# Performer attention and an MLP mixer on one Trainium2 core: q and k of the first two batches loaded in rows of 18 tokens

## The chip, the core and the metric

The kernel runs on one core of a Trainium2 chip. The core has a matrix engine (TensorE, called PE in the profile; its weight loads are listed apart as PEld), a vector engine (VectorE, DVE), a scalar engine (ScalarE, ACT), a general engine (GpSimd, POOL) and SyncE (SP), which here only issues DMAs. Each engine takes its instructions strictly in the order of its program. Matmul results go to eight PSUM banks, and from there ACT or DVE must copy them to SBUF. The metric is the device time of one execution in microseconds, as the median of several runs.

## The reference, cut to what matters

Eight batches of 8 heads, 576 tokens and head size 64 pass through Performer attention (128 random features) and then an MLP mixer.

```python
def phi(x):                                  # x: q or k, scaled by 64 ** -0.25
    proj = np.einsum('bhsd,md->bhsm', x, omega)
    h = proj - np.sum(x * x, -1, keepdims=True) / 2
    return np.exp(h - np.max(h, -1, keepdims=True)) / np.sqrt(m)
kv  = einsum('bhsm,bhsd->bhmd', phi(k), v);  z = phi(k).sum(axis=2)
x   = einsum('bhsm,bhmd->bhsd', phi(q), kv) / (phi(q) . z + 1e-6)     # then (B, 576, 512)
h   = relu(x.T @ w_tok1) @ w_tok2;  u = x + h.T                       # over tokens
out = u + relu(u @ w_ch1) @ w_ch2                                     # over channels, 512 -> 1536 -> 512
```

## The kernel before

Every batch goes through the same stages: transposed q and k (head dimension on the partitions), features (a matmul with omega, then an exponential on ACT, lines 628 and 640 with 499), the maxima of k's features (DVE, 652) and v scaled by them (POOL, 293), kv (PE, 673 and 682), the numerators (PE, 706 and 708), their division (DVE, 715 and 716, for some heads DVE 725 and ACT 728), token mix and channel mix. The 576 tokens are handled as 512 and a tail of 64: a transposed tile keeps 256 columns of main part and 32 columns of tail for each head, two tokens to a column.

Batches 2 to 7 get q and k transposed by DMA through a copy in DRAM. The first two batches (`NPE = 2`) are transposed on PE. For k of batch 0 the main part arrives in fp32 by four DMAs that SP and ACT issue (`load_first`, line 383). All else of these two batches comes by DMAs that POOL issues, and that turn fp32 to fp16 on the way: `load_nat` (317) takes 512 tokens of a head, four to a partition, so that one run in DRAM is 1 KB, and `load_nat_tail` (328) takes the 64 tail tokens of all eight heads. `transposes` (472) turns four heads with eight instructions of 128x128 into one bank, and one copy of 128x1024 (helper line 284) takes it out in the same order; `tail_transposes` (489) needs four instructions and one copy of 128x256 for a whole tail, which puts the columns in order as it copies.

The first batch is the head of the kernel. Its token mix is special (`token_mix_first`): per block of 128 channels a first matmul group (788, 789), a relu, a group that leaves the sum of x and the token mix transposed (800, 802), and a copy of it (tile uT, line 284 again). When three of the four uT copies are done, the first channel matmuls of batch 0 may start (944, three of four contraction blocks), and their fourth block (946) needs the last copy. From there on the channel matmuls of one batch (938, 972, 888) are work that PE can do while the next batch's attention waits for ACT and DVE.

What sets the order is written out by hand. `add` registers jobs, and `Planner.run` issues them as the list `ORDER` says; a negative number is a filler matmul (line 1013) whose result nobody reads. `SLOT` says which bank or buffer each job takes, and `MOVED` puts single jobs on another engine than the usual one. The costs and keys given to `add` no longer decide anything. So the order of a queue (POOL's DMA issues and its arithmetic, ACT, DVE, PE) is fixed, and an instruction that waits holds all behind it on that engine.

## Time and profile before

| what | value |
|---|---|
| median of 3 runs | 279.24 us (278.15 to 279.55) |
| profiled execution: its own time | 279.25 us |
| profiled execution: span from the first to the last instruction | 277.5 us |
| granted TensorE clock, mean | 0.997 |
| PE, DVE, ACT, POOL busy | 97%, 79%, 49%, 34% of the span |
| first channel matmul of batch 0 | 30.06 us |

Times in the profile count from the start of the span; 1.75 us of the execution's time lie outside of it. Busy time of PE counts a matmul until its modelled end, so that neighbours overlap: the step from one 512-column matmul to the next is read off the chain, where eight of line 938 take 1.73 us. In a line of instructions the columns are the start, the duration, the engine, the line, the operation, the tile written and the tile read, their shapes, the number merged into the line, and in brackets the engine's idle time before and what ended it. In a table of stretches each engine has its busy time, with the number of instructions in brackets, and at the end the granted clock, the DMA share and GB/s.

### The profile page before, as it was taken

Reading aid. Unit: us, or ns where it says so; the run is one execution under the profiler, and the core shown is the slowest. Engines: PE = TensorE matmul, PEld = TensorE weight load, DVE = VectorE, ACT = ScalarE, POOL = GpSimd, SP = SyncE. Lnnn points to the kernel's source line nnn. Section 1 sums busy time; section 2 is a strip of 40 time slices with the busy share of each in tenths; the row PEclk is TensorE's granted clock in tenths of the full one; section 3 lists DMA queues with packets and bytes.
Section 4 is the critical chain, followed back from the end, with each engine's and each line's share of the span. In section 5 each row is a group of like instructions: output and inputs, shape, how many; then the busy total and the mean of one; then the engine's idle time right before and its main releaser. Section 6 shows DMA issues by size and latency. Waiting matters only on the chain.

```text
span 277.5 us, 6130 instructions
## 1 busy us (share of the span) xinstructions
PE 269.2 (97%) x2459; PEld 168.2 (61%) x2459; DVE 220.4 (79%) x462; ACT 137.0 (49%) x284; POOL 93.5 (34%) x117
## 2 busy tenths in 40 slices
PE   8989999999999999999999999999999999999992
PEld 4558455445567655756676656655676477456782
DVE  2989678397996999987999799969995991595892
ACT  1988942396595337625756546635744500211200
POOL 8995782063812480076019500600042000000001
PEclk9999999999999999999999999999999999999998
DMA  7999999999999999979999997750342204030125
GB/s 189 174 201 197 208 207 177 197 184 180 204 196 122 218 169 172 192 136 166 180 183 201 234 113 118 171 123 0 102 73 83 90 6 90 0 154 0 76 99 132
DMA packets 84012, 39.66 MB, mean 143 GB/s; under 512 B 64208, under 2 KB 80528, under 8 KB 83792
## 3 DMA queue, kind: packets, MB, share of 16 engines
q0 software_dynamic: 34464, 17.74, 45.8%
q1 hardware_dynamic: 47360, 16.03, 29.1%
q10 hardware_dynamic: 2160, 5.51, 5.1%
q8 instruction: 19, 0.31, 0.5%
q14 instruction: 9, 0.07, 0.1%
HBM read 35.95 MB, written 16.52 MB: 189 GB/s over the span
## 4 chain that ended last, share of the span: by engine, by line
PE 83%; DVE 7%; DMA 4%; POOL 3%; issue 1%; DVEq 0%; POOLq 0%
PE bank L938 30%; PE bank L888 26%; PE bank L749 4%; PE bank L762 4%; DMA r<-in_k_dram 3%; PE bank L673 3%; PE bank L706 3%; PE bank L972 2%; PE bank L640 2%; PE bank L628 2%; DMA vt<-in_v_dram 1%; DVE T L448 1%; DVE km L652 1%; DVE S L293 1%; DVE u L765 1%
## 5 line engine op out<-in xcount | busy, mean ns | idle before, releaser
L938 PE MATMUL bank<-uT,wc 128*128 128x512 f16 x376 | 89.5, 379 | 0.0
L288 ACT ACTIVATE r<-bank 128x512 f16<-128x512 f32 (+1 forms) x86 | 48.2, 601 | 79.0 <-PE bank L938 66.3
L293 POOL TENSOR_TENSOR vs<-v,vs 128x512 f16<-128x512 f16 x32 | 33.6, 1057 | 92.9 <-DVE vs L654 62.8
L938 PEld LDWEIGHTS <-wc 128*128 128x128 f16 x424 | 38.6, 98 | 37.5 <-issue 0.3
L499 ACT ACTIVATE qp<-bank 128x512 f16<-128x512 f32 x64 | 36.8, 625 | 10.1 <-PE bank L640 7.3
L888 PEld LDWEIGHTS <-r 128*128 128x128 f16 x384 | 36.9, 98 | 8.0 <-issue 0.7
L652 DVE TENSOR_REDUCE km<-kp 128x8 f16<-128x1024 f16 x32 | 38.6, 1207 | 2.5 <-ACT kp L499 2.4
L499 ACT ACTIVATE kp<-bank 128x512 f16<-128x512 f32 x64 | 35.8, 615 | 6.3 <-PE bank L628 5.1
L290 DVE TENSOR_SCALAR r<-bank 128x512 f16<-128x512 f32 (+1 forms) x40 | 26.0, 669 | 7.8 <-PE bank L938 6.8
L716 DVE TENSOR_TENSOR x<-bank,rc 128x320 f16<-128x320 f32 x62 | 30.5, 491 | 2.1
L888 PEld LDWEIGHTS <-S 128*128 128x128 f16 x288 | 28.0, 98 | 5.6 <-issue 0.4
L877 DVE TENSOR_TENSOR o<-u,bank 128x512 f32<-128x512 f16 x28 | 19.0, 678 | 7.8 <-PE bank L888 7.7
L888 PE MATMUL bank<-T,r 128*128 128x256 f16 x192 | 23.8, 273 | 0.0
L888 PE MATMUL bank<-T,S 128*128 128x256 f16 x192 | 23.6, 273 | 0.1
L888 PE MATMUL bank<-wc,r 128*128 128x256 f16 x192 | 23.4, 273 | 0.0
L917 POOL DMA_DIRECT2D out_dram<-o x2 | 1.3, 645 | 61.1 <-issue 61.1
L765 DVE TENSOR_TENSOR u<-x,bank 128x512 f16<-128x512 f16 x28 | 17.6, 680 | 4.7 <-PE bank L762 4.7
L877 DVE TENSOR_TENSOR o<-o,bank 128x512 f32<-128x512 f32 (+1 forms) x27 | 16.5, 615 | 3.1 <-PE bank L888 2.6
L706 PEld LDWEIGHTS <-qp 128*128 128x128 f16 x256 | 13.8, 98 | 7.9 <-DVE kvsb L284 0.2
L706 PE MATMUL bank<-kvsb,qp 128*128 128x65 f16 x256 | 15.5, 193 | 0.0
L715 DVE RECIPROCAL rc<-bank 128x5 f32<-128x5 f32 x62 | 11.5, 185 | 4.8 <-PE bank L708 3.5
L673 PEld LDWEIGHTS <-kp 128*128 128x128 f16 x256 | 11.0, 98 | 5.2 <-DVE o L284 1.0
(117 smaller groups left out, 381.5 us busy)
## 6 DMA issues: line engine op xcount, KB each, us to landing
out_dram<-o ACTq DMA_DIRECT2D x9, 512.0 KB, 3.5
q<-in_q_dram POOLq DMA_DIRECT2D x6, 576.0 KB, 9.6
wc<-in_moe_w_ch_dram POOLq DMA_DIRECT2D x4, 768.0 KB, 13.4
k<-in_k_dram POOLq DMA_DIRECT2D x6, 512.0 KB, 8.1
v<-in_v_dram POOLq DMA_DIRECT2D x6, 512.0 KB, 10.1
out_dram<-o SPq DMA_DIRECT2D x5, 512.0 KB, 3.3
r<-in_q_dram POOLq DMA_DIRECT2D x4, 256.0 KB, 7.3
v<-in_v_dram POOLq DMA_DIRECT2D x4, 256.0 KB, 8.0
```

Of the source, the lines that this page charges most:

```text
L288: nc.scalar.activation(out=out, in_=in_, func=AF.Relu)
L290: nc.vector.tensor_relu(out=out, in_=in_)
L293: (nc.gpsimd if eng == "POOL" else nc.vector).tensor_tensor(**kw)
L499: nc.scalar.activation(out=out, in_=in_, func=AF.Exp, bias=0.0, scale=1.0)
L652: nc.vector.reduce_max(out=mx, in_=kpv, axis=AX.X)
L673: nc.tensor.matmul(ps[:, i, :], kpv[:, 2 * i + j // 2, j % 2, :], vs[:, i * NJ + j, 0 : D + 1], start=(i == 0 and j == 0), stop=False, ski ...
L706: nc.tensor.matmul(ps[:, k, j * 65 : (j + 1) * 65], st, s[:, i, 0 : D + 1], start=True, stop=True)
L716: nc.vector.tensor_tensor(out=t_x[place("x", b)][:, :, (2 * hp + hs[0]) * D : (2 * hp + hs[0] + n) * D].rearrange("p j (i d) -> p i j d", ...
L765: nc.vector.tensor_tensor(out=t_u[place("u", b)][:, j, :], in0=t_x[place("x", b)][:, j, :], in1=bank(n), op=ALU.add)
L877: nc.vector.tensor_tensor(out=o, in0=a, in1=ps, op=ALU.add)
L888: nc.tensor.matmul(ps[:, j * DH : (j + 1) * DH], a[:, cb, j * P : (j + 1) * P], w[:, cb, :], start=(bank_of(b, j0) not in held and j == j0 ...
L938: nc.tensor.matmul(ps, wc1[:, db, cb * P : (cb + 1) * P], moving(db), start=(db == 0), stop=(db == ND - 1))
```

## The change

q of batch 0, and q and k of batch 1, are no longer split into main part and tail when loaded. Four heads are 2304 tokens, and they are laid as 128 rows of 18 tokens (`RW = 18`), so that one run in DRAM is 4.5 KB and one head covers 32 partitions. Three tail loads of `load_nat_tail` go, and the one load of k of batch 1 becomes two of four heads. k of batch 0 stays as it was, with its tail.

The new function `row_transposes` takes the place of `transposes` and `tail_transposes` for them. It issues nine pairs of transposes per four heads, each from 64 partitions and 128 columns, the two of a pair on the two halves of the partitions and into two banks. Each bank holds two heads, and the copy out of it (128x576) puts the columns in order: neighbours in the output lie 64 columns apart in the bank. For k a second, small copy brings the tail columns (128x64) to the tile that the tail's matmul reads. The matmuls that read these tiles now pick tokens in steps of two columns, as they do in batches 2 to 7. Jobs that depended on one copy of four heads now depend on the copy of their two heads, and the tail's matmul (601, and 534 for batch 1) on all copies.

With it `ORDER`, `SLOT` and `MOVED` are new. In the list of before, ACT has ten exponentials of batch 1 (two of them of the tail) ahead of the copy of uT's last block, and does two of the four uT copies by then; in the new list it has nine of them, and does only that one. New on ACT ahead of it are two of the four row copies of q of batch 0, three of the four of k of batch 1, two of the four of q of batch 1, the copy of k's tail of batch 0 and one more relu; DVE no longer does these, but does the first and third uT copies, one vs product (formerly POOL's), and the other row copies. On DVE and ACT k of batch 0 is copied by two each, not three and one. On POOL the list of loads starts with the tail of k, q, the two loads of v's tail, q, v, the second half of k of batch 1, v, and its first half. On PE the first kv matmuls of batch 0 come before the transposes of batch 1, which came first; there are 22 fillers in place of 20; and two q feature groups of batch 1 that stood ahead of the first channel matmul stand behind it. Later batches have the same jobs with neighbours swapped here and there, and some relus and copies on the other of ACT and DVE.

```diff
 ORDER = [
-    6, 5, 0, 2, 3, 1, 4, 17, 15, 19, 7, 10, 13, -1, -2, -3, -4, -5, -6, -7, 49, 12, 40, 47, 8, 41, 43, 42, 48,
-    23, 44, 50, -8, 45, 11, 108, 9, 123, 110, 51, 52, 22, 125, 46, -1, -4, 71, 124, 79, 14, 53, 72, 109, 32, 93,
-    81, 57, 54, 95, 18, 55, 114, 58, 80, 30, 76, 67, 77, 20, 56, 74, -7, -7, -7, 96, 85, 73, 82, 75, 94, 97, -4,
-    111, 68, 83, 99, 126, 112, 98, 21, -2, -2, 199, 78, 129, 86, -3, 63, 128, 84, 100, -8, 87, 201, 64, 88, 16,
...
+    6, 5, 0, 2, 3, 1, 4, 16, 14, 18, 15, 7, 10, 9, -1, -2, -3, -4, -5, -6, -7, 47, 8, 45, 38, 48, 39, 12, 46,
+    40, 41, 11, 106, 42, 43, 107, 22, 108, 49, 44, 77, 13, 50, 121, 78, 112, 91, 21, 123, -8, 51, 79, 17, 52,
+    53, 28, 93, 83, -1, -4, -3, -1, 94, 122, 19, 80, 96, 54, 73, 92, 69, 55, 81, 70, 82, 95, 24, 56, 97, 71, 84,
+    -5, -8, -3, -5, -7, -7, -8, -1, 74, 109, 72, 127, 76, 98, -6, -2, 85, 75, 124, 63, 113, 86, 125, 128, 87,
+    89, 110, 99, 90, 30, 126, 114, 88, 100, 129, 20, 65, 57, 130, 111, 64, 25, 133, 131, 59, 135, 115, 31, 58,
+    132, 104, 60, 23, 134, 136, 101, 116, 61, 118, 137, 29, 102, 119, 103, 105, 33, 147, 117, 120, 139, 138,
...
 MOVED = {
-    52: "DVE", 70: "ACT", 88: "ACT", 142: "DVE", 144: "DVE", 146: "DVE", 148: "ACT", 152: "ACT", 155: "DVE",
-    158: "DVE", 176: "DVE", 178: "DVE", 182: "ACT", 192: "ACT", 216: "ACT", 244: "DVE", 258: "DVE", 288: "DVE",
-    326: "ACT", 380: "DVE", 401: "DVE", 428: "DVE", 430: "DVE", 434: "DVE", 436: "DVE", 486: "DVE", 500: "DVE",
...
+    42: "DVE", 46: "ACT", 48: "ACT", 52: "ACT", 56: "ACT", 58: "ACT", 59: "ACT", 61: "ACT", 62: "ACT", 65:
+    "ACT", 86: "ACT", 128: "DVE", 138: "DVE", 142: "DVE", 144: "DVE", 150: "ACT", 156: "DVE", 160: "DVE", 162:
+    "DVE", 164: "ACT", 172: "ACT", 176: "DVE", 180: "ACT", 214: "ACT", 286: "DVE", 324: "ACT", 378: "DVE", 399:
...
 }
...
     NPE = 2
+    RW = S * 4 // P
     c_scale = float(1.0 / math.sqrt(math.sqrt(D)))
...
         for i, w in enumerate("qk"):
-            nat[w, b] = flat(t)[:, i * H * 256 : (i + 1) * H * 256].rearrange("p (h e) -> p h e", h=H)
-        nat["t", b] = flat(t)[:, 2 * H * 256 : 2 * H * 256 + H * D].rearrange("p (i e) -> p i e", i=4)
+            nat[w, b] = flat(t)[:, 2 * i * RW * D : 2 * (i + 1) * RW * D].rearrange("p (g e) -> p g e", g=2)
+        nat["t", b] = flat(t)[:, 4 * RW * D : 4 * RW * D + H * D].rearrange("p (i e) -> p i e", i=4)
 
...
             nc.gpsimd.dma_start(
-                out=nat[w, b][:, h0:h1, :],
-                in_=src[w][b, h0:h1, 0:SM, :].rearrange("h (p j) d -> p h (j d)", j=NJ),
+                out=nat[w, b][:, h0 // 4, :],
+                in_=src[w][b, h0:h1].rearrange("h s d -> (h s d)").rearrange("(p f) -> p f", p=P),
             )
...
     load_nat(0, "q", 4, 8, -8.5)
-    load_nat_tail(0, "q", -8.48)
     load_v(0, -8.45, (), 4, 8)
...
     load_wc1(0)
-    load_nat(1, "k", 0, 8, -9.61)
-    load_nat_tail(1, "k", -3.48)
+    load_nat(1, "k", 0, 4, -9.61)
+    load_nat(1, "k", 4, 8, -9.61)
     load_v_tail(1, -3.46)
     load_wc1(1)
-    load_nat_tail(1, "q", -3.44)
     load_w1t(0, -3.42)
...
         t = (t_qT if w == "q" else t_kT)[place(w + "T", b)]
-        return (t[:, 0 : H * R] if w == "k" and b >= NPE else t).rearrange("p (h r) -> p h r", h=H)
+        return (t[:, 0 : H * R] if w == "k" and b != 1 else t).rearrange("p (h r) -> p h r", h=H)
 
...
 
-    def transposes(b, w, h0, h1, key, on_act=False, key_out=None):
-        name = ("t", w, b, h0)
-        first = b == 0 and w == "k"
+    def transposes(b, h0, h1, key, on_act=False, key_out=None):
+        name, w = ("t", "k", b, h0), "k"
         def go():
-            ps = bank(name) if first else bank16(name)
-            what, ident = (first_k, ident32) if first else (nat[w, b], ident16)
+            ps = bank(name)
             for i in range(2 * (h1 - h0)):
                 h, pr = h0 + i // 2, i % 2
-                nc.tensor.transpose(ps[:, i * P : (i + 1) * P], what[:, h, pr * P : (pr + 1) * P], ident)
+                nc.tensor.transpose(ps[:, i * P : (i + 1) * P], first_k[:, h, pr * P : (pr + 1) * P], ident32)
         def out_():
             n = h1 - h0
-            ps = (bank(name) if first else bank16(name))[:, 0 : n * R].rearrange("p (h r) -> p h r", h=n)
-            copy(eng, rows_of(b, w)[:, h0:h1, 0:R], ps)
+            copy(eng, rows_of(b, w)[:, h0:h1, 0:R], bank(name)[:, 0 : n * R].rearrange("p (h r) -> p h r", h=n))
         take = [("bank", name), (w + "T", b)]
-        t = add("PE", mm(2 * (h1 - h0), P) * (2 if first else 1), key, go, deps=[ld[w, b, h0], j_ident32 if first else j_ident], take=take)
+        t = add("PE", mm(2 * (h1 - h0), P) * 2, key, go, deps=[ld[w, b, h0], j_ident32], take=take)
         eng = engine("ACT" if on_act else "DVE")
...
             tr[w, b, h] = e
+
+    def row_transposes(b, w, g, key, on_act=False, key_out=None):
+        names = [("t", w, b, g, o) for o in range(2)]
+        def rows():
+            for i in range(RW // 2):
+                for o in range(2):
+                    p = slice(o * ST, (o + 1) * ST)
+                    nc.tensor.transpose(bank16(names[o])[:, i * ST : (i + 1) * ST], nat[w, b][p, g, i * P : (i + 1) * P], ident16[p, p])
+        t = add("PE", mm(9, 64), key, rows, deps=[ld[w, b, 4 * g], j_ident], take=[*[("bank", n) for n in names], (w + "T", b)], rows=True)
+        for o in range(2):
+            eng = engine("ACT" if on_act else "DVE")
+            def rows_out(o=o, eng=eng):
+                h = 4 * g + 2 * o
+                to = rows_of(b, w)[:, h : h + 2, :]
+                copy(eng, to.rearrange("p h (c i) -> p h c i", i=RW // 2), bank16(names[o])[:, 0 : 2 * RA].rearrange("p (i h c) -> p h c i", i=RW // 2, h=2))
+                if w == "k":
+                    copy(eng, t_ktt[place("ktt", b)][:, h * RT : (h + 2) * RT].rearrange("p (h r) -> p h r", h=2), to[:, :, R:RA])
+            e = add(eng, 0.38 if w == "q" else 0.48, key if key_out is None else key_out, rows_out, deps=[t], take=[("ktt", b)] if w == "k" else [], give=[("bank", names[o])])
+            for h in range(2):
+                tr[w, b, 4 * g + 2 * o + h] = e
 
...
             ps = bank16(name)[:, 0 : H * RT].rearrange("p (i h g) -> p h g i", i=4, h=H)
-            to = t_ktt[place("ktt", b)].rearrange("p (h r) -> p h r", h=H) if w == "k" else rows_of(b, "q")[:, :, R:RA]
+            to = t_ktt[place("ktt", b)].rearrange("p (h r) -> p h r", h=H)
             copy(eng, to.rearrange("p h (g i) -> p h g i", g=8), ps)
-        t = add("PE", mm(4, 64), key, go, deps=[ld[w + "t", b], j_ident], take=[("bank", name), ("ktt", b) if w == "k" else ("qT", b)], rows=True)
+        t = add("PE", mm(4, 64), key, go, deps=[ld[w + "t", b], j_ident], take=[("bank", name), ("ktt", b)], rows=True)
         eng = engine("ACT" if on_act else "DVE")
...
             if dma_in:
-                return ld[w + "T", b]
-            return tr[w + "t", b] if h is None else tr[w, b, h]
+                return [ld[w + "T", b]]
+            return list(dict.fromkeys(tr[w, b, x] for x in (range(H) if h is None else h)))
 
...
             t = rows_of(b, w)[:, h, 0:R]
-            return t.rearrange("p (c r) -> p r c", r=2) if dma_in else t.rearrange("p (r c) -> p r c", r=2)
+            return t.rearrange("p (c r) -> p r c", r=2) if b else t.rearrange("p (r c) -> p r c", r=2)
 
...
             return [("bank", (n, e)) for e in range(2)]
-        if dma_in:
-            j_ktt = ld["kT", b]
-        else:
-            j_ktt = tr["kt", b]
+        j_ktt = [tr["kt", b]] if b == 0 else src_of("k")
         def kt():
...
-                            st = (st.rearrange("p (c r) -> p r c", r=2) if dma_in else st.rearrange("p (r c) -> p r c", r=2))[:, j // 2, :]
+                            st = st.rearrange("p (c r) -> p r c", r=2)[:, j // 2, :]
                             nc.tensor.matmul(ps[:, k, j * 65 : (j + 1) * 65], st, s[:, i, 0 : D + 1], start=True, stop=True)
...
     for i in range(4):
-        transposes(0, "k", 2 * i, 2 * i + 2, HEAD["kx"][i], BY["kx"][i] == "A", HEAD["kxo"][i])
+        transposes(0, 2 * i, 2 * i + 2, HEAD["kx"][i], BY["kx"][i] == "A", HEAD["kxo"][i])
     tail_transposes(0, "k", HEAD["ktx"], BY["ktx"] == "A", HEAD["ktxo"])
     for i in range(2):
-        transposes(0, "q", 4 * i, 4 * i + 4, HEAD["qx"][i], BY["qx"][i] == "A", HEAD["qxo"][i])
-    tail_transposes(0, "q", HEAD["qtx"], BY["qtx"] == "A", HEAD["qtxo"])
-    for h0, h1 in ((0, 4), (4, 8)):
-        transposes(1, "k", h0, h1, KEYS["l1"] + 0.1 * h0)
-        transposes(1, "q", h0, h1, KEYS["l1"] + 0.1 * h0 + 0.01)
-    tail_transposes(1, "k", -0.55)
-    tail_transposes(1, "q", -0.55)
+        row_transposes(0, "q", i, HEAD["qx"][i], BY["qx"][i] == "A", HEAD["qxo"][i])
+    for i in range(2):
+        row_transposes(1, "k", i, KEYS["l1"] + 0.4 * i)
+        row_transposes(1, "q", i, KEYS["l1"] + 0.4 * i + 0.01)
 
...
```

More of the change, by code (lines that the diff above doesn't have):

```diff
@@ L103 @@
+    1148: "DVE", 1150: "DVE", 1152: "DVE", 1160: "DVE", 1200: "SP", 1205: "ACT", 1206: "SP", 1207: "ACT", 1208:
+    "SP",
 }
@@ L534, in kt @@
                     nc.tensor.matmul(ps[e][:, g * M : (g + 1) * M], t[half[e], g * P : (g + 1) * P], omT[half[e]], start=True, stop=True)
-        j_kt = add("PE", mm(2, P), k0, kt, deps=[j_ktt, j_omT], take=[*two_of(n_kt), ("kpt", b)], give=[("kT" if dma_in else "ktt", b)], rows=True)
+        j_kt = add("PE", mm(2, P), k0, kt, deps=[*j_ktt, j_omT], take=[*two_of(n_kt), ("kpt", b)], give=[("kT" if dma_in else "ktt", b)], rows=True)
         if b == 0:
@@ L601, in qt @@
                 nc.tensor.matmul(ps[e][:, 0:256], omT[half[e]], t[half[e], :, R:RA], start=True, stop=True)
[L602 removed]
+        j_qt = add("PE", mm(1, 256), kqt, qt, deps=[*src_of("q"), j_omT], take=[*two_of(n_qt), ("qpt", b)], give=[("qT", b)], rows=True)
         j_qte = []
@@ L628, in kp @@
                             nc.tensor.matmul(ps[e][:, c : c + M], m[half[e], r, :], omT[half[e]], start=True, stop=True)
-            j_k = add("PE", mm(4, P), at_["kp"], kp, deps=[src_of("k", hh[0]), src_of("k", hh[1]), j_omT], take=[("bank", (n_k, 0)), ("bank", (n_k, 1)), ("kp", (b, hp))], rows=True,
+            j_k = add("PE", mm(4, P), at_["kp"], kp, deps=[*src_of("k", hh), j_omT], take=[("bank", (n_k, 0)), ("bank", (n_k, 1)), ("kp", (b, hp))], rows=True,
                       give=[("kT", b)])
```

30 lines of the change are left out of this document (14 added, 16 removed), and 108 rows, old and new, of the table ORDER.

## The prediction

> **What bounds the kernel now.** I read the page's slices first, then the chain in order of time, then busy time by stretch, then the instructions of the first 31 us.
>
> ```profile
> PE   8989999999999999999999999999999999999992
> ACT  1988942396595337625756546635744500211200
> ```
>
> PE is full from the second slice to the last but one, so whatever reaches the end of the kernel must change how much PE has done by some early moment. ACT is nearly full only in the first fifth. The chain starts on POOL's issues and one load:
>
> ```profile
> 7.55 0.66 POOL vt L349
> 8.21 8.51 DMA r<-in_k_dram
> 16.77 0.62 PE bank L472 x8
> 30.13 0.75 PE bank L944 x3
> ```
>
> (Start, duration, what.) The load of batch 1's k lands at 16.7 and holds PE; from 16.77 PE follows PE. But fillers and stretched waits are in that. By stretch:
>
> ```profile
> 7.00:14.00 7.00, 6.45 (x83) 3.76 (x82) 6.32 (x12) 6.60 (x16) 6.87 (x10) 1.00 1.40 175
> 14.00:21.00 7.00, 6.18 (x99) 4.26 (x98) 5.94 (x16) 6.18 (x16) 6.98 (x9) 1.00 1.36 201
> 21.00:28.00 7.00, 7.00 (x109) 5.63 (x107) 6.38 (x20) 5.99 (x19) 4.19 (x6) 1.00 1.27 197
> 35.00:42.00 7.00, 7.00 (x80) 4.13 (x79) 5.24 (x11) 2.65 (x6) 5.93 (x7) 1.00 1.26 208
> ```
>
> (Stretch, its length, busy PE, PEld, DVE, ACT, POOL, clock, DMA share, GB/s.) From 7 to 28 us DVE has 18.6 and ACT 18.8 of 21 us; from 35 on ACT is mostly idle. So ahead of the channel matmuls three things are tight together, loads, DVE and ACT, and the change takes from the first and gives to the other two. The instructions that price it:
>
> ```profile
> 8.52 0.42 DVE L284 COPY ktt<-bank 128x256 f16<-128x256 f16 x1 [0.61 <-PE bank L489]
> 10.17 0.69 DVE L284 COPY qT<-bank 128x1024 f16<-128x1024 f16 x1
> 10.93 0.37 ACT L284 COPY qT<-bank 128x256 f16<-128x256 f16 x1
> 20.66 1.17 ACT L728 ACTIVATE x<-bank,rc 128x64 f16<-128x64 f32 x5
> 28.52 0.59 ACT L284 CAST uT<-bank 128x512 f16<-128x512 f32 x1
> 30.06 0.82 PE L944 MATMUL bank<-uT,wc 128*128 128x512 f16 x3
> 55.88 4.11 ACT L499 ACTIVATE kp<-bank 128x512 f16<-128x512 f32 x8
> 56.44 0.96 PE L628 MATMUL bank<-omT,kT 64*128 64x128 f16 x24
> 62.23 0.64 DVE L284 COPY o<-bank 128x512 f32<-128x512 f32 x1
> 62.93 0.42 PE L673 MATMUL bank<-vs,kp 128*128 128x65 f16 x8 [0.54 <-DVE o L284]
> ```
>
> **The change part by part.**
>
> *Loads.* Three tail issues of about 0.6 us leave POOL and one k issue (0.94) becomes two (about 0.6 each: the tail and q issues lie at 0.58 to 0.80). Ahead of POOL's first product there are 13 issues, not 15, so it starts near 10.6, not at 12.76. The second half of batch 1's k is POOL's eighth load, not its eleventh. The bytes ahead of its end fall from 4.0 to 3.6 MB in DRAM, and before they took 4.1 to 16.7: it lands near 15.3. It is no longer waited for, since PE has it after the first kv. Longer runs may raise the rate (160 to 175 GB/s while 1 KB runs load, 192 to 213 later): this only widens a margin that is already there, priced at nothing. Without that cover PE waits at its transposes, at most as it did, until 16.8.
>
> *PE.* Gone are 48 transposes of 128 columns (0.45 per eight in the chain, 2.7) and 12 of tails (24 to 38 ns apart, 0.4): 3.1. New are 108 small ones in pairs. Half the columns of the paired 128-column matmuls above (24 in 0.79, first to last start: 30 ns) would be 15 ns each, 1.6; their full 30 ns gives 3.2. The tails come as near as 24 ns: I take that, 2.6, a gain of 0.5 (bounds: 1.5 gained, 0.1 lost).
>
> The Trainium skill, TensorE: Matmul & The Clock Gate, section "Wait — 56ns, not 53.3ns?", states that matmuls never start closer than about 25 ns, which would make 2.7 of it; it also states that with hardware decode off about 62 ns go to each, which would make 6.7, and speaks against the change. The 30 ns above show that the second does not hold in this trace.
>
> *Copies.* A 256-element copy that reorders took DVE 0.42 and ACT 0.37, one of 1024 in order 0.69 on DVE. The reordering one runs at an element per cycle: by the 130-column copy (0.30) and the 256 one the slope is 0.95 ns per element, so 576 cost DVE 0.73; at the rate of 1024 in order 0.42 would do, the low end. ACT: from 256 (0.37) and 512 (0.59) elements, 0.64 alone, some 0.54 back to back, as eight exponentials take 4.11. For k a second copy follows that reads what the first wrote: 0.1 of gap as between the maximum and the reciprocal on DVE, and 0.23 as one of the five 64-element pieces: 1.0 in all on ACT (bounds 0.74 with no gap, 1.1). Together the copies grow from 5.3 us (six of 0.69, one of 0.42 and two of 0.37) to about 9.5, in a stage where both engines are near full. The vs product that moves to DVE costs it at most 0.6 (768 elements take 0.55 there) and POOL is rid of 1.06: POOL was last with it at 19.66, ACT is last now.
>
> *The path.* I sum what ACT must do before the last uT copy ends. Before: 16 exponentials of batch 0 at 0.52 (8.3), four of k's tail (1.15), two of q's tail (1.55), one tail copy (0.37), two kvsb (0.54), two relus (0.8), two divisions (2.3), ten exponentials of batch 1 (8 x 0.52 and 0.93, 5.1), two uT copies (1.2): 21.3, from 7.92 on gives 29.2. The trace has 29.11: ACT sets this point. After: the same 8.3, 1.15, 1.55, 0.37, 0.54 and 2.3, three relus (1.2), nine exponentials of batch 1 (4.2 and 0.35), one uT copy (0.58), and new two q copies of batch 0 (1.1), three of batch 1's k (3.0), two of its q (1.1): 25.7. The start is earlier: with two k copies on ACT only omT (6.72) and a first feature group (0.55 to its exponential) stand ahead, 7.3. So the last copy ends at 33.0 (bounds with the cheaper and dearer copies: 32.1 and 33.5). DVE, by the same adding, has its three uT copies done near 30, PE reaches the first channel matmuls near 30.3, does two groups of three (1.3) and waits for the fourth block until 33.0.
>
> Before, PE did 2.94 us of channel matmuls from 30.06 to 33.0. After, it has done 1.3, has two q groups of 0.22 of batch 1 still to do, and 0.5 less transposing behind it: 2.94 - 1.3 + 0.43 - 0.5 = 1.6 late. The 0.8 us earlier kv and the wait that went at 16.77 are inside this: PE is ahead until about 18, and gives it back waiting for ACT.
>
> Of that something returns. At 62.93 kv of batch 2 waits for DVE's output copy, which stands behind a weight difference (T, 1.64 at 59.24); PE loses 0.7. The new list puts that difference behind the output copies. I take 0.6 (0 to 0.7). The remaining swaps in later batches I take as nothing, within 1 us either way, from the 6 us that PE lies above its columns (203.3 at 0.216 us per 512) between 63.24 and 272.6.
>
> Sum against the profiled execution: 279.25 + 1.6 - 0.6 = 280.25, so **280.2**; that execution lies on the median of the runs.
>
> **The rivals.**
>
> *ACT's lateness spreads (slower).* From 33.0 ACT has batch 1's other exponentials and now eight relus of batch 0's channel blocks, not six. Up to its last exponential of q's tail that is some 7.9 us, to 40.9; PE's order reaches batch 1's first kv after 7.2 us, 40.2. Each channel block keeps a bank until its relu, and exponentials keep two: PE stops whenever its bank's relu is late. For: ACT was busy 5.8 of 6 us from 30 to 36 already. Against: it was idle most of 36 to 50. Price up to 1.5, and the 0.6 not regained: 279.25 + 1.6 + 1.5 = 282.3.
>
> *The order wins (faster).* Everything of batch 1 stands about 3 us earlier among PE's work: its token mix comes after 33.1 us of columns, not 36.7. If ACT catches up by 42, the tight place at 56 to 63 dissolves and later batches, which all start from it, keep 2 of the 6 us mentioned. For: ACT's idle time from 36 to 50. Against: later batches lose the same at each stage, and nothing in them changes. 279.25 + 1.6 - 0.7 - 2.0 = 278.1. It decides if the wait for the fourth block is over by about 32.
>
> *The rows gain nothing, or cost at PE.* Loads do not land sooner: 280.2 all the same, since nothing waits for them. If the two halves of a pair do not overlap and each small transpose costs what one of 128 columns does, 56 ns, the 72 in PE's tight stretch cost 32 more each: 2.3, so 282.5. The Trainium skill's second figure, on the same page, would make this 2.7.
>
> **How the numbers follow.** Half a per cent, 1.4 us, is about what a measurement here can tell from none: slower starts at 280.65, faster below 277.85. Chances: my forecast 0.42 (own range 279 to 281.3), the spreading 0.30 (280.9 to 283.2), the order 0.23 (276.8 to 279), unpaired transposes 0.03, others 0.02. Slower: a quarter of the forecast's 0.42 (0.10), nearly all of the spreading, and 0.03: 0.41. Faster: most of the order's, 0.18. Same: 0.41. The range leaves out a third of the order's chance and a quarter of the spreading's: 277.3 to 282.8.
>
> **What would show it.** Copies of 128x576: 0.73 on DVE, 0.64 on ACT. First exponential near 7.3, the last uT copy's end near 33.0 on ACT with no idle time before it, a wait of PE at line 946. k's second half landed before PE's transposes of it. No wait at 62.9. I am wrong if ACT idles between 8 and 32, if the row copies take half the time, or if the first channel matmuls come at 29 or earlier with 946 right behind.

## The result, and the profile after

The changed kernel takes 278.11 us (median of 20 runs, 277.57 to 279.2), the kernel before 279.12 (20 runs). The ratio is 0.9969 with a 95% interval of 0.9957 to 0.9981: 0.3% faster, where 0.4% slower was forecast. One of the 20 runs of the kernel before, 282.81 us, is a slow one and is left out of the ratio. The time lies near that of the rival in which the order wins (278.1). The profiled execution of after took 278.63 us, with a span of 276.8.

Busy time in 40 slices, after:

```profile
PE   7999999999999999999999999999999999999993
ACT  3999973288595237835756446635754500031200
```

PE stays full. ACT is at nine tenths or more in four slices running; before, two of these were at eight. The chain in order of time (start, duration, what) shows ACT from 9 to 25 us, then PE, with 1.4 us of DVE's copies at 27.54 between:

```profile
9.34 1.12 ACT kp L516 x2
...
14.44 0.53 ACT qT L286
...
19.55 0.24 ACT ktt L286
...
22.72 2.06 ACT x L742 x10
...
25.11 0.38 PE bank L642 x7
...
27.54 0.69 DVE uT L286
...
30.30 1.29 PE bank L958 x6
31.60 0.22 PE bank L960
```

Before, the load of k (until 16.77) stood in this place. The last two lines are batch 0's first channel matmuls and their fourth block: it follows without a wait. By stretch (busy PE, PEld, DVE, ACT, POOL, then clock, DMA share, GB/s):

```profile
14.00:21.00 7.00, 6.65 (x140) 4.63 (x140) 6.46 (x15) 6.94 (x18) 6.18 (x9) 1.00 1.16 202
21.00:28.00 7.00, 6.67 (x116) 5.16 (x109) 4.58 (x13) 6.93 (x23) 3.77 (x5) 1.00 1.14 204
```

ACT has 13.9 of 14 us from 14 to 28 (12.2 before). The instructions that answer the forecast's prices:

```profile
7.63 1.09 ACT L516 ACTIVATE kp<-bank 128x512 f16<-128x512 f32 x2 [0.48 <-PE bank L642]
19.52 0.75 DVE L286 COPY kT<-bank 128x576 f16<-128x576 f16 x1
22.09 0.63 ACT L286 COPY qT<-bank 128x576 f16<-128x576 f16 x1
30.34 0.59 ACT L286 CAST uT<-bank 128x512 f16<-128x512 f32 x1
63.82 0.42 PE L687 MATMUL bank<-vs,kp 128*128 128x65 f16 x8
```

The first exponential starts at 7.63 (forecast 7.3), the last uT copy ends at 30.93 (forecast 33.0), kv of batch 2 starts at 63.82 with no idle time ahead of it.

**Where PE lost time.** To compare positions I count, at a mark, the time less the columns that PE has done by then: 0.417 ns a column and 2.5 ns a matmul, which make 0.216 us for 512 columns and 0.056 for 128, the steps of the chain (1.73 for eight, 0.22 for four). Matmuls that run in pairs on half the array count half; the fp16 transposes of q, k and their tails and the fillers count as nothing. The number is what PE has lost so far, in us of the profiled execution; it serves to compare kernels, and executions with the same head differ by up to 0.5 at the first mark. The last three columns are experiments told of below.

| mark | before | after | before, T moved | after, T put back | after, late part old |
|---|---|---|---|---|---|
| batch 0's first channel matmul | 18.04 | 18.55 | 17.64 | 18.52 | 18.61 |
| first token mix group of batch 1 | 18.48 | 19.25 | 18.09 | 19.23 | 19.32 |
| first token mix group of batch 2 | 20.49 | 20.51 | 19.49 | 20.83 | 20.57 |
| first tail features of batch 3's k | 21.17 | 20.95 | 20.17 | 21.28 | 21.67 |
| last tail group of the token mix | 26.00 | 25.65 | 24.92 | 25.99 | 26.36 |

After is 0.5 us late at the first channel matmul (forecast 1.6), still 0.8 late at batch 1's token mix, level at batch 2's, and 0.35 ahead at the end.

### The profile page after: what moved, and what is told of

The parts are those of the page before. It is cut to its first block, busy times and chain, and to the rows that moved or that the text cites. A ratio compares the mean times of both kernels' runs of the same rounds, so it can differ in the third digit from the quotient of the medians.

```text
span 276.8 us, 6243 instructions
## 1 busy us (share of the span) xinstructions
PE 269.2 (97%) x2509; PEld 167.5 (61%) x2509; DVE 219.2 (79%) x458; ACT 141.1 (51%) x296; POOL 90.2 (33%) x114
## 4 chain that ended last, share of the span: by engine, by line
PE 87%; ACT 7%; DVE 3%; DMA 1%; issue 1%; ACTq 0%
PE bank L952 32%; PE bank L902 27%; PE bank L763 5%; PE bank L776 5%; PE bank L642 3%; PE bank L654 3%; PE bank L986 2%; PE bank L687 2%; PE bank L720 2%; ACT qp L516 2%; DMA wc<-in_k_dram 1%; DVE x L730 1%; PE bank L470 1%; ACT kp L516 1%; PE bank L830 1%; ACT r L290 1%
## 5 line engine op out<-in xcount | busy, mean ns | idle before, releaser
L290 ACT ACTIVATE r<-bank 128x512 f16<-128x512 f32 (+1 forms) x89 | 48.9, 599 | 82.5 <-PE bank L952 67.8
L295 POOL TENSOR_TENSOR vs<-v,vs 128x512 f16<-128x512 f16 x31 | 32.7, 1060 | 91.8 <-DVE vs L668 62.5
L292 DVE TENSOR_SCALAR r<-bank 128x512 f16<-128x512 f32 (+1 forms) x37 | 24.6, 677 | 8.4 <-PE bank L952 7.5
```

Source lines behind the costliest of these rows:

```text
L290: nc.scalar.activation(out=out, in_=in_, func=AF.Relu)
L292: nc.vector.tensor_relu(out=out, in_=in_)
L295: (nc.gpsimd if eng == "POOL" else nc.vector).tensor_tensor(**kw)
```

## The experiments

Theory 1: ACT's queue sets the head, as forecast, but the new work on it is smaller than I summed; and the regain at 56 to 63 us comes from the weight difference T. Theory 2, formed from the table: PE's order in the later batches has a part too. Rivals stand with each run. Each ratio is to the kernel before, timed beside that run; a difference between two kernels is the difference of their ratios, times 279 us.

**T put back, and T moved alone.** The second difference (job 35 in the new list, 37 in the old) goes ahead of the second maximum again; and in the kernel before, it alone goes behind the third.

```diff
 after_T_ahead, ORDER of after:
-..., 459, 185, 342, ..., 391, 281, 35, 392, 388, ...
+..., 459, 185, 35, 342, ..., 391, 281, 392, 388, ...
 before_T_behind, ORDER of before:
-..., 359, 392, 37, 372, ..., 378, 363, 393, ...
+..., 359, 392, 372, ..., 378, 363, 37, 393, ...
```

> The changed kernel with one DVE job put back: the second weight difference (T) stands again between the output copy at 59.24 us and the second maximum of batch 2, as before the change. Theory 1 (the regain at 56 to 63 us comes from this move): T takes 0.95 to 1.6 us there, the third output copy ends at about 63.8 in place of 62.8, kv of batch 2 waits for it again, 0.5 to 0.7 us of PE are lost and kept to the end: 278.7, ratio 0.998 to the kernel before. Rival (the gain comes from the new rows and the order of the head, T was hidden either way): 278.1, ratio 0.997, no wait of PE near 63.

> The kernel before with that one move alone: the second T goes behind the maximum that starts at 62.79. Theory 1: the wait of 0.54 us at 62.93 goes, 0.5 to 0.7 us are gained to the end: 278.5, ratio 0.998. Rival: something else is late in its place (T's next reader, or the bank of another copy), the wait moves a few us further on and the time stays 279.1, ratio 1.000.

Measured: after with T put back 278.53 us, ratio 0.9986 (0.9977 to 0.9996); before with T moved 278.32, ratio 0.9979 (0.997 to 0.9988). The timelines of DVE and PE, first after with T back:

```profile
59.77 1.69 DVE L448 TENSOR_TENSOR T<-wc,T 128x1536 f16<-128x1536 f16 x1
63.51 0.62 PE L830 MATMUL bank<-r,w 128*64 128x512 f16 x4 [0.20 <-DVE o L286]
```

then before with T moved:

```profile
61.93 0.42 PE L673 MATMUL bank<-vs,kp 128*128 128x65 f16 x8
63.05 0.94 DVE L448 TENSOR_TENSOR T<-wc,T 128x1536 f16<-128x1536 f16 x1
```

With T back, the second maximum starts at 61.38, and a wait on the output copy returns (0.20, one instruction ahead of kv, which starts at 64.16). With T moved in the old kernel, kv follows its neighbours at once, and T itself takes 0.94 in its new place, not 1.64. The move is worth 0.5 us in the new kernel (the two intervals touch) and 0.6 in the old; theory 1 holds, and 0.6 was the forecast.

**More and less on ACT.** In after_act_plus three row copies on ACT are made twice. In after_ktt_once the four small copies of k's tail columns become one on DVE, where it idled.

```diff
 after_act_plus, in rows_out:
+                if (b, w, g, o) in ((0, "q", 1, 1), (1, "k", 0, 0), (1, "k", 0, 1)):
+                    copy(eng, to.rearrange("p h (c i) -> p h c i", i=RW // 2), bank16(names[o])[:, 0 : 2 * RA].rearrange("p (i h c) -> p h c i", i=RW // 2, h=2))
 after_ktt_once, in rows_out:
+                if (b, w, g, o) == (1, "q", 1, 0):
+                    copy("DVE", t_ktt[place("ktt", 1)].rearrange("p (h r) -> p h r", h=H), rows_of(1, "k")[:, :, R:RA])
...
-                if w == "k":
-                    copy(eng, t_ktt[place("ktt", b)][:, h * RT : (h + 2) * RT].rearrange("p (h r) -> p h r", h=2), to[:, :, R:RA])
```

> The changed kernel with three row copies on ACT made twice (one of q of batch 0, two of k of batch 1): 3 x 0.54 = 1.6 us more on ACT between 14 and 21 us, nothing else changed. Theory 1: the first channel matmul comes 1.6 us later, near 31.9, and 1.0 to 1.6 us reach the end: 279.4, ratio 1.001. Rival (ACT is not what sets this point, PE and DVE follow only partly): below 0.5 us later, 278.5, ratio 0.998.

> The changed kernel with the four small copies of k's tail columns (three on ACT, 0.24 us a step; one on DVE, 0.33) made into one 128x256 copy on DVE, in the 0.9 us that DVE idles at 24.1. Theory 1 (ACT, step by step, sets when batch 0's channel matmuls start, and PE keeps what it gains there): ACT's chain is 0.7 us shorter, the first channel matmul starts near 29.6 in place of 30.30, and 0.3 to 0.7 us of it reach the end: 277.6, ratio 0.995. Rival (ACT's lead is lost at the next tight place): the first channel matmul is earlier, the end is not: 278.1, ratio 0.997.

The one copy takes 0.22 on DVE. Measured: 279.87 us with the doubled copies, ratio 1.0038 (1.0025 to 1.005), so 1.9 us over after for 1.6 added (1.4 to 2.4 by the intervals); 277.37 us with the one small copy, ratio 0.9947 (0.9935 to 0.9959), so 0.6 under after for 0.72 taken away (0.1 to 1.1). The lines of after_ktt_once:

```profile
7.13 1.08 ACT L516 ACTIVATE kp<-bank 128x512 f16<-128x512 f32 x2 [0.49 <-PE bank L642]
29.06 0.58 ACT L286 CAST uT<-bank 128x512 f16<-128x512 f32 x1
```

From first exponential to the end of the last uT copy it takes 22.51 us, against 23.30 in after. In both directions what ACT gets or loses here, between 14 and 22 us, reaches the end of the kernel, as closely as the intervals tell. This kernel beats both.

**The same load in the kernel before.** Three exponentials of batch 0's q are made twice.

```diff
                     exp(t_qp[place("qp", (b, hp))][:, e, :], bank((n_q, e)))
+                    if b == 0 and (hp, e) in ((0, 0), (2, 0), (1, 1)):
+                        exp(t_qp[place("qp", (b, hp))][:, e, :], bank((n_q, e)))
```

> The kernel before with three exponentials of batch 0's q on ACT made twice, 3 x 0.5 = 1.5 us more between 13.7 and 17 us, the same kind of load as was added to the changed kernel (1.6 us there). The prediction's step (ACT without idle time sets the last uT copy in the kernel before): all 1.5 us reach the first channel matmul and the end: 280.6, ratio 1.005. Rival (ACT had 2.2 us of idle time between 8 and 29 us in the kernel before, so it did not set this point alone): at most 0.8 us: 279.1 to 279.9, ratio 1.000 to 1.003.

Measured: 280.7 us, ratio 1.007 (1.0041 to 1.01), 1.9 us more: all of the 1.5 comes through, within the interval. So ACT's exponentials up to some 17 us do set the first channel matmul in the kernel before (31.45 in place of 30.06), though ACT idles behind them. ACT's timeline of the kernel before shows where:

```profile
18.00 0.27 ACT L284 CAST kvsb<-bank 128x130 f16<-128x130 f32 x1 [0.30 <-PE bank L682]
18.79 0.27 ACT L284 CAST kvsb<-bank 128x130 f16<-128x130 f32 x1 [0.52 <-PE bank L682]
...
27.55 0.58 ACT L284 CAST uT<-bank 128x512 f16<-128x512 f32 x1 [0.46 <-PE bank L802]
```

With 0.20 at 23.00 and 0.34 at 25.23 these are 1.82 us of waits for PE and DVE. PE's timeline of the kernel with the added load shows that PE in its turn waits for ACT just ahead of that:

```profile
15.60 0.59 PE L1015 MATMUL bank<-S 128*128 128x512 f16 x2 [0.72 <-ACT qp L499]
17.84 0.38 PE L1015 MATMUL bank<-S 128*128 128x512 f16 x1 [0.85 <-ACT qp L499]
```

Behind 17.84 PE shows no idle time until the first channel matmul; in the kernel before it shows none from 16.77 to 30.06. So ACT's exponentials decide when this unbroken run of PE begins, and inside the run it is ACT that waits: its gaps of 0.20, 0.34 and 0.46 come again, all 1.4 us later. My rival fell for work ahead of the run. All of the added load stood there, and no run adds work to ACT inside the run, where its idle time lies; that this time was free is argued, not shown. The row copies of batch 1 that the change gives to ACT (18.62 to 25.6) stand there. In after, ACT has less than 0.3 us of gaps from its first exponential to the last uT copy.

**Rows without the new order.** The list of before is kept; each old copy of four heads becomes a copy of two heads on DVE and one on ACT, the tails' jobs go, and the tail features that need all row copies stand later.

```diff
 rows_old_order, ORDER of before (-, its numbers) in the new numbers (+; transposes, then copies):
-..., 53, ..., 54, ..., 59, ..., 60, ...
+..., 51, ..., 52, 53, ..., 57, ..., 58, 59, ...
 rows_old_order, MOVED:
+    53: "ACT", 56: "ACT", 58: "ACT", 61: "ACT", 65: "ACT", 68: "ACT",
```

> The new loads, row transposes and copies alone, with the order of jobs of the kernel before: each old copy of four heads becomes a copy of two heads on DVE and one on ACT; the tails' jobs go; only the tail features of batch 0's q and of batch 1's k stand later, since they now need all row copies. Theory 1 (ACT's queue is what the new copies are paid with): ACT gets six copies and two small ones for two tail copies, some 3.0 us more, less 2.2 us of idle time that it has there: the first channel matmul 0.8 to 2 us later than in the kernel before, 279.1 + 0.8 to 1.5 = 280.2, ratio 1.004. Rival (the rows pay by themselves: 1.6 us less transposing, two issues less ahead of POOL): faster than before also in the old order, 278.3, ratio 0.997.

Measured: 282.94 us, ratio 1.013 (1.01 to 1.016), 3.9 us slower than before and 4.8 slower than after: worse than theory 1's 1.5. PE's timeline shows two of its waits:

```profile
12.56 0.28 PE L614 MATMUL bank<-qT,omT 64*128 64x256 f16 x2 [1.58 <-DVE qT L285]
24.48 0.29 PE L547 MATMUL bank<-omT,ktt 64*128 64x128 f16 x4 [0.66 <-DVE kvsb L285]
```

They are for DVE, and another of 0.55 at 27.03 is for ACT's division: the tail features wait for all four row copies. One of the small copies also met a product of POOL that had begun 0.04 us before it, and took 1.05, where the other on DVE takes 0.20:

```profile
18.75 1.05 DVE L285 COPY ktt<-kT 128x64 f16<-128x64 f16 x1
```

In the old list the rows cost time; the whole change, with the new list, does not. Some of the 3.9 may be due to banks: the row transposes need two where the old ones had one, and 20 other tiles lie in other banks than before.

**Unpaired transposes.** Nine on one half of the partitions, then nine on the other.

```diff
-            for i in range(RW // 2):
-                for o in range(2):
+            for o in range(2):
+                for i in range(RW // 2):
```

> The changed kernel with the row transposes issued half by half: nine on the first 64 partitions, then nine on the others, so that neighbours share their rows and cannot overlap. Theory 1 (pairs overlap in full, 13 ns from start to start; ACT sets the head's end): a start every 25 to 30 ns, 18 in 0.45 to 0.55 us in place of 0.32, but PE has idle time there and ACT's chain hardly moves: 278.1 + 0 to 0.4, ratio 0.997 to 0.998. Rival (PE's transposing is itself what was saved): all of 108 x 12 to 17 ns, 1.3 to 1.8 us, comes back: 279.6, ratio 1.002.

Measured: 277.92 us, ratio 0.9958 (0.9942 to 0.9974): no loss. Weight loads of one group of 18, unpaired:

```profile
18.87 0.48 PEld L487 LDWEIGHTS <-r 64*128 64x128 f16 x18
```

and in after:

```profile
19.20 0.32 PEld L487 LDWEIGHTS <-r 64*128 64x128 f16 x18
```

A single load takes some 0.10, so starts are (0.32 - 0.10) / 17 = 13 ns apart in pairs and 22 ns unpaired. Over 108 that is 1 us of PE, and it does not show in the time: while the transposes ran, the kernel was not waiting for PE.

**The load of k.** In the kernel before, the transposes that waited for it go behind the first kv.

```diff
 before_k_later, ORDER of before:
-..., 129, 86, -3, 63, 128, 84, 100, -8, 87, 201, ...
+..., 129, 86, -3, 128, 84, 100, -8, 87, 63, 201, ...
```

> The kernel before with the first transposes of batch 1's k put behind the first kv of batch 0 on PE, as the change has it; loads and all else as before. In the profile of before PE waits there 0.49 us (16.28 to 16.77) for the load; in that of the kernel with T alone moved the load came 1 us sooner and PE did not wait. If the wait sets the first channel matmul: 0.3 to 0.5 us faster, 278.7, ratio 0.9985. The prediction's step (PE is ahead until about 18 and gives it back waiting for ACT, so the wait is worth nothing): 279.1, ratio 1.000.

Measured: 279.01 us, ratio 1.0001 (0.9992 to 1.001): nothing. In its profiled execution PE's first kv is then held by something else at the same time, POOL's product:

```profile
17.50 0.40 PE L673 MATMUL bank<-vs,kp 128*128 128x65 f16 x8 [0.27 <-POOL vs L293]
```

The load's 8.51 us were the longest step in the chain of before, and the wait behind them was worth nothing.

**DVE and POOL beside ACT.** The fourth vs product goes back to POOL, alone, together with the one small copy, and with that and a row copy of q moved from ACT to DVE; the last kernel has the one small copy and another row copy of q on DVE, with the vs product left on DVE.

```diff
 after_vs_pool, and after_ktt_vsp (with the one small copy), in MOVED:
-    ..., 86: "ACT", 128: "DVE", 138: "DVE", ...
+    ..., 86: "ACT", 138: "DVE", ...
 after_ktt_vs, the same and:
-    ..., 52: "ACT", 56: "ACT", 58: "ACT", ...
+    ..., 52: "ACT", 58: "ACT", ...
 after_ktt_q (with the one small copy, vs on DVE), job 61 from ACT to DVE (six tiles change banks with it):
-    ..., 116, 61, 118, ..., 139, 138, 326, ...
+    ..., 116, 118, ..., 139, 138, 61, 326, ...
```

> The changed kernel with the fourth vs product of batch 0 back on POOL: DVE loses 1.16 us at 16.53, POOL gets 1.06 after 17.09, and its loads behind that are issued 1.06 later. If POOL's product then ends at 18.15 in place of DVE's 17.69, the fourth kv and what follows on PE are up to 0.46 us later: 278.1 to 278.6, ratio 0.997 to 0.9985. Rival (DVE was as tight as ACT, so its relief counts): 277.6, ratio 0.995.

> The changed kernel with k's small copies as one on DVE and with the fourth vs product of batch 0 on POOL, no copy of q moved. The two alone gave 0.9947 and 0.9957. If ACT's 0.72 us and DVE's 1.16 us count apart from each other: 277.0, ratio 0.993. If either relief is used up by the other's engine: 277.4, ratio 0.995.

> The changed kernel with k's small copies as one on DVE, the fourth vs product on POOL, and the second ACT copy of batch 0's q (0.53 us at 13.93) on DVE. Theory 1 (what ACT does ahead of its first kvsb copy near 16.8 decides when PE's unbroken work begins): 0.2 to 0.5 us faster than with the one small copy alone: 276.9 to 277.2, ratio 0.993. Rival (DVE's maxima, 0.75 us later, and POOL's product take over): 277.4 to 278.1, ratio 0.995 to 0.997.

> The changed kernel with the four small copies of k's tail columns as one on DVE, and with one more row copy of batch 1's q (the one on ACT at 22.1 us) moved to DVE behind the first uT copy: ACT loses 0.72 and 0.53 us of its chain, DVE gets 0.35 + 0.75 us where it idled 0.9. Theory 1: the first channel matmul near 28.9 to 29.2 with a first exponential at 7.63, and 0.3 to 0.5 us more than with the one small copy alone: 276.9 to 277.1, ratio 0.993. Rival (DVE is now as tight as ACT, its next uT copy and relu come later by as much): no gain over the one small copy, 277.4, ratio 0.995.

Measured: 277.64 (0.9957, 0.9944 to 0.997), 277.65 (0.995, 0.9935 to 0.9966), 277.78 (0.9957, 0.9942 to 0.9971) and 278.1 (0.9959, 0.9942 to 0.9975). The vs product on POOL costs nothing and may gain a little; none of the four beats the one small copy alone. In the last one ACT waits 0.47 at 21.28 for DVE's reciprocals. In after_ktt_vsp PE waits for two loads:

```profile
44.32 1.04 PE L985 MATMUL bank<-wc,r 128*128 128x512 f16 x4 [1.07 <-DMA wc<-in_moe_w_ch_dram]
56.71 0.29 PE L547 MATMUL bank<-omT,kT 64*128 64x128 f16 x4 [0.56 <-DMA kT<-k]
```

That execution took 279.47, 1.8 us over the median of its kernel, so these waits are not those of its usual runs. With ACT relieved, DVE is as tight, by the wait in the last kernel; why the vs product on POOL adds nothing to the one small copy stays open.

**The late part.** Up to the first token mix group of batch 2 each kernel keeps its own list; from there on it takes the other's order. Of the engines only PE's order differs there, in 107 places. The banks and buffers (`SLOT`) go with an order: the first two runs take the other kernel's, as far as they are free (463 of the 472 places of that part, and 468 of 469), the two with _b keep their own, and after_late_banks keeps the new order and takes the old places (309 of 717 change, 250 of them banks, the others buffers in SBUF). The edits in words:

```diff
 after_late_old, after_late_old_b:
-ORDER of after
+ORDER of after up to 397, then the rest in the order of before
 before_late_new, before_late_new_b:
-ORDER of before
+ORDER of before up to 399, then the rest in the order of after
 after_late_banks, SLOT of after:
-from 397 on the banks of after
+from 397 on the banks of before where these are free
```

> The changed kernel up to the tail group of batch 2's token mix (75.85 us), and from there PE's order of the kernel before (some 100 PE jobs swap places with neighbours; the other engines' orders are the same in both). Theory 2 (part of the gain is PE's order in batches 2 to 7: in the traces PE loses 5.1 us beside its columns from there to the last tail group with the new order, 5.4 to 5.5 with the old): 0.25 to 0.37 slower than the changed kernel, 278.4, ratio 0.998. Rival (no part of the gain; the prediction's step): 278.1, ratio 0.997.

> The kernel before up to the tail group of batch 2's token mix (76.04 us), and from there PE's order of the changed kernel. Theory 2: 0.25 to 0.37 faster, 278.8, ratio 0.999. Rival: 279.1, ratio 1.000.

> As after_late_old (the changed kernel up to batch 2's first token mix group, from there PE's order of the kernel before), but with the banks and buffers of the changed kernel: 20 of 717 places differ from it, where after_late_old took 308 from the old list or by default. If PE's late order is what the 0.8 us came from: 278.8, ratio 0.9995. If it was the banks (PE waited 0.44 at 80.80 for a bank that ACT held, in the same order of instructions as in the changed kernel up to there): 278.1, ratio 0.997.

> The changed kernel with its own order throughout, and from batch 2's first token mix group on the places of the kernel before where these are free (309 of 717 differ). If the banks are what cost 0.8 us in after_late_old: 278.8, ratio 0.9995, with a wait of PE near 80.8 again. If PE's late order did: 278.1, ratio 0.997.

> The kernel before with PE's new order from batch 2's first token mix group on and its own banks (48 of 717 places differ). If the new late order is worth something by itself, and before_late_new lost it again by mixed banks: 278.7, ratio 0.9985. If neither order nor banks of the late part matter to the old first part: 279.1, ratio 1.000.

Measured:

| kernel | us | ratio | interval |
|---|---|---|---|
| after_late_old | 278.79 | 0.9997 | 0.9982 to 1.0012 |
| before_late_new | 279.21 | 1.0009 | 0.9997 to 1.0021 |
| after_late_old_b | 282.12 | 1.0112 | 1.0096 to 1.0129 |
| after_late_banks | 283.23 | 1.0162 | 1.0143 to 1.0181 |
| before_late_new_b | 283.86 | 1.0179 | 1.0161 to 1.0197 |

I had expected differences below 1 us in all five. The three in which an order has places that were chosen for another are 4.0 to 5.4 slower than the kernel that they came from. The clearest is after_late_banks, which issues what after issues in the same order and only uses other banks and buffers: 5.4 us slower than after. PE's timeline in it:

```profile
80.74 0.38 PE L642 MATMUL bank<-omT,kT 64*128 64x128 f16 x7 [0.44 <-ACT qp L516]
104.66 1.02 PE L952 MATMUL bank<-uT,wc 128*128 128x512 f16 x4 [0.49 <-ACT r L290]
```

Each, and one of 0.39 at 125.02, is a wait of PE for ACT or DVE, put down to a bank that they have yet to empty. From 76 us on PE shows 2.4 us of idle time here and none in after; the rest of the 4.6 by which the profiled spans differ does not show as idle time. Banks and buffers were not changed apart. The first is there in after_late_old too (0.44 at 80.80), whose instructions up to there are those of after.

Order and banks together: the old late part behind the new first part loses 0.8 us against after, the new late part behind the old first part gains nothing. By the table it all happens at the seam. From batch 2's mix to batch 3's tail features PE loses 0.44 in after, 1.10 with the old late part, 0.68 in before; from there to the last mark 4.70, 4.69 and 4.83. So theory 2 holds only in this form: the new late part's places spare the new first part a wait at 80.8; behind it the later batches differ by no more than 0.14.

## Why the prediction was wrong, step by step

**Loads: right.** POOL's first product starts at 10.58 (10.6), the second half of batch 1's k lands at 13.3 (15.3), the transposes of k wait for nothing, and before_k_later shows that the wait that went was worth nothing. What held kv in its place, in that run's profiled execution, was POOL's product (0.27), not ACT as I had written.

**PE's transposes: size off, without effect.** 108 at 13 ns are 1.4 us; I took 2.6. The gain is 1.7, just past my bound of 1.5. The run without pairs shows that this did not matter. (The 30 ns that I read off the paired feature matmuls are 33: 24 starts in 0.75.)

**Copies: right one by one.** 0.75 on DVE (0.73), 0.63 on ACT alone (0.64), 0.53 in the chain (0.54). The pair for k takes 0.80, not 1.0: the small copy adds 0.24, with a gap of 0.02. The vs product on DVE takes 1.16, where I had at most 0.6.

**The path: this step failed.** I wrote: "21.3, from 7.92 on gives 29.2. The trace has 29.11: ACT sets this point." That the sum met the trace was luck, and the sum for after, 25.7, inherited two errors.

The first is in the terms. Apart from the exponentials and the q copies, I added durations, where the queue goes by steps from one start to the next. In after's chain an exponential takes 0.49 (I had 0.52), a division of two heads 2.06 (2.3), a relu 0.28 to 0.38 (0.4), a kvsb copy 0.12 to 0.17 (0.27), k's pair 0.80 (1.0), q's two tail exponentials 1.23 (1.55).

The second is the path: I took ACT's queue as full from 7.92 to 29.11. It held 19.4 us of work and 1.8 of waits, not 21.3 of work. ACT sets the point only up to some 17 us, as the doubled exponentials show; from 16.77 to 30.06 PE shows no idle time, the chain follows PE, and ACT waits for it. The copy that ends at 29.11 is not the last in time either: ACT's third, of another block that the first channel matmul needs, ends at 29.87. The same head in before_T_behind has its first exponential 0.21 later (8.14) and its first channel matmul 0.40 sooner (29.66), so the one does not follow from the other. In after's head it does: 22.5 us lie between them in after (7.63 and 30.14) and in after_late_old_b (7.13 and 29.65).

After holds 23.0 us of work and 0.3 of waits. So the work grew by 3.7, not 4.4, and 1.5 of it took the place of waits that I did not know of: the stretch grew by 2.1. The last copy ends at 30.93, 2.1 sooner than summed, and the wait of PE at the fourth block did not come. None of the signs that I had named for being wrong came either; none of them tested the sum for before.

The Trainium skill, ScalarE: Activation LUTs, section "What ACT_TABLE_LOAD costs", says that back-to-back ACTIVATEs overlap by about 93 ns. The trace agrees: 0.60 each, 0.49 from start to start, and 0.63 against 0.53 for the row copies.

**The regain: right.** 0.6 forecast; 0.5 and 0.6 by the two runs on T.

**"The remaining swaps in later batches I take as nothing": right from batch 3 on, not at the seam.** Behind 84 us PE loses 4.7 us with either late part. At 76 to 84 after loses 0.24 less than before, and loses 0.66 more with the old late part. The bound of 1 us either way held, but I had looked at orders alone and not at banks.

**The sum.** Forecast were 1.6 for the head, 0.6 back at T, nothing later: +1.0. By the ratio, after is 0.9 faster. T is 0.5 of it, and by the table 0.2 to 0.4 lie behind batch 2's mix. The head then costs about nothing. In the table it costs 0.5, but after's profiled execution, 0.5 over its median, started late (below): at the first channel matmul the same head had lost 18.1 in after_late_old_b, and that of before 17.6 to 18.2 in four executions. Another reading of the runs gives it more: after_late_old, the new first part with T moved, is level with the kernel before (0.9997), where T moved alone gives 0.9979; head and seam together cost 0.5 there. So the head costs between nothing and 0.5, not 1.6, and that is most of the miss of 1.9.

The rival "the order wins" named the condition that came true (the fourth block's wait over by 32; there was none) and the time. The time is luck: its reason, an ACT that catches up by 42 and later batches that keep 2 us, is not what happened. ACT was not late, and the later batches keep 0.2 to 0.4.

Left open: how the head's share splits between rows and order, since the old list with the new rows differs in banks and tail jobs too.

## What to carry to other kernels

A queue is summed by the steps from one start to the next, as the chain has them, not by durations, and a sum that meets the trace is only proved when the engine's idle time in that stretch is counted as well. Whether an engine sets a point is asked by adding a known load to it, and the answer holds for the place of the load: here both kernels passed on all of it, but in the kernel before it stood ahead of ACT's 1.8 us of idle time. An order of work and its assignment of banks and buffers are one design: the same instructions in the same order, with other places, were 5.4 us slower.

## What the runs showed of the hardware

Transposes on the two halves of the partitions overlap: 13 ns from start to start of their weight loads, and 22 unpaired. The Trainium skill, TensorE: Matmul & The Clock Gate, section "Wait — 56ns, not 53.3ns?", has starts never closer than about 25 ns; the trace differs, and the measurement decides. The Trainium skill, TensorE: Matmul & The Clock Gate, section "The mechanism", says that a weight load overlaps matmuls in flight on other rows; the pairs agree.

The first eight transposes, the same code in every kernel here, take from 1.06 to 1.94 us. After, and after_unpaired:

```profile
4.58 1.94 PE L470 MATMUL bank<-S,wc 128*128 128x128 f32 x8 [0.22 <-DMA wc<-in_k_dram]
```

```profile
4.61 1.06 PE L470 MATMUL bank<-S,wc 128*128 128x128 f32 x8 [0.39 <-DMA wc<-in_k_dram]
```

With them the first exponential moves: it starts between 6.69 and 7.68 in after and the kernels made from it. The granted clock reads 1.00 all through, though seven fillers ahead of the transposes step by 0.43 and later ones by 0.22. The Trainium skill, TensorE: Matmul & The Clock Gate, section "What's actually happening", says that PE runs at half rate until a free-running window of some 3.4 us was busy, so that the moment varies by half a microsecond either way; the trace agrees, with half the rate at first and transposes that vary by 0.9. After's profiled execution was one that started late; of after and the kernels made from it the four with 1.94 lie 0 to 0.6 over their medians.

A weight difference of 1536 elements on DVE took 0.94 with POOL silent, and 1.64 to 1.69 when a product of POOL had begun some 0.2 us before it. In before_T_behind the difference began first, at 63.05, and took 0.94; there the product that began inside it took longer, 1.62 in place of 1.07:

```profile
63.29 1.62 POOL L293 TENSOR_TENSOR vs<-v,vs 128x512 f16<-128x512 f16 x1 [0.40 <-DVE vs L654]
```

The vs product on DVE took 1.16 in after, with one of POOL's running beside it for its first 0.6.
